# Attention and two MoE layers on one core: four bit passes, P.V halves for two heads at once, the 1e-9 on GpSimd, seven score tiles, another first pair

## The chip, the core and the metric

The kernel runs on one core of one Trainium2 chip. The metric is the device time of one execution in microseconds (us). Before the change it is 682.02 us, the median of three runs (681.51 to 682.46).

## What is computed

Attention over 2 batches x 8 heads, 768 positions, head width 64, and behind it two dense layers. A query sees only keys with the same six sign bits:

```python
q_bits = (np.einsum('bhsd,dk->bhsk', q, proj) > 0)
k_bits = (np.einsum('bhsd,dk->bhsk', k, proj) > 0)
mask = bucket(q_bits)[:, :, :, None] == bucket(k_bits)[:, :, None, :]
scores = np.where(mask, scale * q @ k.T, -1e9)
attn = np.exp(scores - scores.max(-1, keepdims=True))
x = (attn / (attn.sum(-1, keepdims=True) + 1e-9)) @ v      # then heads side by side: 1536 x 512
h = np.maximum(np.maximum(x @ w1, x @ w2), x @ w3) @ w_out
g = h @ w_in; out = (g * sigmoid(1.702 * g)) @ w_out2
```

## The kernel before

Every fp32 product is made of fast fp32r passes over a high and a low part (`hi` rounded to fp32r, `lo` what is left). Work comes in eight pairs of heads, 16 heads, and 96 units of 128 queries by all 768 keys of a head.

*Preparation of a pair.* K and Q of both heads are loaded as one tile [128, 6, 2, 64], turned by TensorE (line 287) in four pieces of three transposes, and split into `kq` high (ScalarE, lines 296 and 298) and low (VectorE, 302 and 304). `prep_bits` then multiplies them with the projection, two pieces of six passes of 384 columns (line 314): for K and for Q, projection high by data high, high by low, low by high. Rows 0 to 43 of the result belong to K, rows 64 to 107 to Q, twelve rows a head: six projections, twice. VectorE turns them into bits and their opposites (line 320), GpSimd scales the Q half by -2^100 (line 325). `prep_stack` copies the parts into `kst` and `qst` by eight transfers on SP's queue (line 335), so that two passes of S = Q.K contain the scores and, in 12 extra rows, 2^100 for every bit that differs.

*The first pair* goes its own way to be early (`solo_` functions): 64-row transposes (line 355), copies of parts by GpSimd (368), a bit piece of two passes per half and operand (384 on 128 rows, 385 on 64 rows), the bits by VectorE (389), the scale by ScalarE (393). Ahead of it TensorE runs nine matmuls of zeros (`WARM`, line 251), and fillers of the same kind (1448) where the plan leaves TensorE idle in the first 26 us.

*A unit.* S in four passes (416); VectorE clamps and takes the minimum (423); ScalarE takes exp with the row sum (429). For every two units: VectorE adds 1e-9 to the sums (433) and inverts them (434), GpSimd scales both score tiles (437), TensorE transposes them in three groups of four (446), ScalarE copies the high part (452), VectorE makes the low part (456), and P.V runs in two halves of six passes (464) on weights [V high | V low]. The result has the product with V high in rows 0 to 63 and with V low in rows 64 to 127. ScalarE copies it (485), a transfer brings the other half to the head's own rows (490), GpSimd adds the two (495, 64x256), and when both heads are there splits the sum into `xh` (501) and `xl` (503), the input of the MoE.

*What sets the order.* `task` gives each step a due time (`DUE`) and a cost (`COST`); `plan` picks, among the steps whose operands and buffers (`free`) are ready, the one with the smallest start + LAM x due. The order that comes out is written to each engine's queue and is fixed there (`in_order`). Engines run their queues in order. Score tiles (`se`) number six, S tiles two, T tiles three, P.V one. The MoE behind has an order of its own, in which TensorE runs without waits.

Of the kernel before, what the change touches and what calls it, by code (L numbers as in the profile page):

```python
# [6 lines left out]
F32R = mybir.dt.float32r  # L7
# [8 lines left out]
BIG = float(2.0 ** 100)  # L16

# [4 lines left out]
SEB = 6  # L22
WARM = 9

DUE = {'prep0': 1.56, 'pa0': -7.67, 'pd0': -16.75, 'prep1': 4.13, 'pa1': -6.11, 'pd1': 4.98, 'S': 0.66, 'clamp': 0.12,
       'exp': 2.96, 'recip': 1.32, 'scale': -4.24, 'T': 3.7, 'hi': 2.96, 'lo': 4.88, 'PV': 7.17, 'xc': 5.17, 'xa': 11.13, 'xs': -8.82,
       'prep': 1.09, 'pa': -6.93, 'pd': -0.18, 'sb': -18.87, 'v': 12.02, 'raw': 3.68, 'stack': 2.09, 'w': 3.14}

COST = {'S': ('PE', .70, .95), 'clamp': ('DVE', .87, 1.05), 'exp': ('ACT', .93, 1.12), 'recip': ('DVE', .14, .36),
        'scale': ('POOL', .92, 1.0), 'T': ('PE', .437, .66), 'hi': ('ACT', .485, .63), 'lo': ('DVE', .60, .73),  # L30
        'PV': ('PE', .72, .95), 'xc': ('ACT', .30, .42), 'xm': ('SP', .65, 3.2), 'xa': ('POOL', .73, .78),
        'xs': ('POOL', 1.2, 1.25),
        'prep': ('PE', .33, .6), 'bits': ('PE', 1.05, 1.32), 'pa': ('ACT', .40, .55), 'pd': ('DVE', .47, .62),
        'pdb': ('DVE', .52, .7), 'sb': ('POOL', .52, .6), 'v': ('POOL', 1.6, 1.65), 'raw': ('SP', 1.4, 5.5),
        'stack': ('SP', 6.6, 9.5), 'none': ('NONE', 0.0, 0.0), 'wm': ('ACT', .57, .7), 'wc': ('POOL', .7, .8),
        'wb': ('DVE', 1.25, 1.4), 'ws': ('ACT', .52, .68), 'wl': ('POOL', 1.27, 1.33), 'up': ('PE', 2.72, 3.0),
        'solob': ('PE', .36, .62), 'dup': ('POOL', .5, .6), 'sbits': ('DVE', .6, .72), 'slow': ('PE', .65, 1.0), 'spd': ('DVE', .52, .62), 'cold': ('PE', .64, 1.0), 'raw0': ('SP', .7, 3.8), 'raw00': ('SP', 2.1, 4.6),
        'project': ('DVE', 1.2, 1.3),
        'warm': ('PE', 4.4, 4.4), 'wraw': ('SP', .45, 6.0)}

FILL = 26.0
LAM = 0.05
# [157 lines left out]
def build(tc, q, k, v, proj, w1, w2, w3, w_out, m2_in, m2_out, out):  # L200
# [13 lines left out]
    NR = D + 44  # L214
# [28 lines left out]
    def f32(ap):  # L243
        return ap.bitcast(F32)


    warm = st([P, 512], "warm", 1, BF16)
# [8 lines left out]
    for base, fill in ((-102, 1.0), (-96, 0.0), (-70, 1.0), (-38, 0.0), (-32, 1.0), (-6, 0.0)):  # L256
        nc.gpsimd.affine_select(out=off, in_=off, compare_op=ALU.is_ge, fill=fill, base=base,
                                pattern=[[0, 1]], channel_multiplier=1)
    pf = st([P, NA], "pf", 1)
    pdf = st([P, 2, NR], "pdf", 1)  # L260
    pdt = st([P, 4, NR], "pdt", 1, F32R)
    nc.gpsimd.memset(pdf, 0.0)
    pds = st([P, 4, D + NA], "pds", 1, F32R)
    offk = st([NR, 1], "offk", 1)
    nc.vector.tensor_scalar(out=offk, in0=off, scalar1=-1.0, scalar2=1.0, op0=ALU.mult, op1=ALU.add)
# [42 lines left out]
    def prep_bits(g, a, get):  # L308
        s = slice(a * HALF, (a + 1) * HALF)
        o = get()[:NR, :HALF]  # L310
        terms = [(pdt[:, i, :], kq[g, name][z][:, s])
                 for x, name in enumerate("kq") for i, z in ((x, 0), (x, 1), (2 + x, 0))]
        for n, (w, x) in enumerate(terms):
            nc.tensor.matmul(o, w, x, start=(n == 0), stop=(n == len(terms) - 1))  # L314
        if a == 0:
            aug[g] = st([NR, S], "aug", 2, F32R)
        t = aug[g]

        def on_dve():
            nc.vector.tensor_scalar(out=t[:, s], in0=o, scalar1=0.0, scalar2=off, op0=ALU.is_gt, op1=ALU.subtract)  # L320
        return (lambda: None), on_dve

    def scale_bits(g, s):
        t = aug[g][D:NR, s]
        nc.gpsimd.tensor_scalar(out=t, in0=f32(t), scalar1=-BIG, scalar2=1.0, op0=ALU.mult, op1=ALU.mult)

    def prep_stack(g, j):
# [3 lines left out]
        ra = slice(32 * j, 32 * j + NA)  # L331
# [12 lines left out]
        last = dma(qs[D:D + NA, 1, :], aug[g][D + 32 * j:D + 32 * j + NA, :])  # L344
# [6 lines left out]
    def solo_transpose(j, name, a, get):  # L351
        t = qkv_raw[0, name]
        o = get()
        for c in range(3):
            nc.tensor.transpose(o[:D, c * P:(c + 1) * P], t[:, 3 * a + c, j, :], ident)
# [23 lines left out]
    def solo_bits(j, name, a, get):  # L379
# [5 lines left out]
        nc.tensor.matmul(o, pds[:D, 2 * x + 1, :], t[:D, z, s], start=False, stop=True)  # L385
# [45 lines left out]
    def softmax_recip(jq):  # L431
        rc[jq] = st([P, 2], "rc", 4)
        nc.vector.tensor_scalar_add(sm[jq], sm[jq], 1e-9)
        nc.vector.reciprocal(rc[jq], sm[jq])  # L434

# [31 lines left out]
    def x_place(jq):  # L467
# [3 lines left out]
        own = slice(j * D, (j + 1) * D)  # L471
        oth = slice((1 - j) * D, (2 - j) * D)
        return g, j, i, b, p, own, oth, slice(i * 2 * P, (i + 1) * 2 * P)

    xtmp = {}

    def x_copy(jq):
        g, j, i, b, p, own, oth, s = x_place(jq)
        if j == 0 and i == 0:
            xf[g] = st([P, S], "xf", 1)  # L480
        if not X:
            X[0] = (st([P, EC, B * S], "xh", 1, F32R), st([P, EC, B * S], "xl", 1, F32R))
        xt, xm = (st([P, 2 * P], tag, 3) for tag in ("xt", "xm"))
        xtmp[jq] = (xt, xm)
        nc.scalar.copy(xt, pv[jq])

    def x_move(jq):
        g, j, i, b, p, own, oth, s = x_place(jq)
        xt, xm = xtmp[jq]
        nc.sync.dma_start(xm[own, :], xt[oth, :])  # L490
# [995 lines left out]
```

## Time and profile before

| | |
|---|---|
| median of 3 runs | 682.02 us |
| profiled execution | 681.95 us |
| its span (first to last instruction) | 680.0 us |
| busy TensorE / VectorE / ScalarE / GpSimd | 673.8 / 581.9 / 424.4 / 312.2 us |
| attention ends, MoE alone on TensorE | 245.51 us |

The span is what the trace covers; the 1.95 us around it are outside. A busy time counts an engine as busy from an instruction's start to its end; TensorE's instructions overlap, so its pace is read from the chain, where a piece is the time by which it moved the end. Line numbers are those of the code above. PE is TensorE, DVE VectorE, ACT ScalarE, POOL GpSimd, SP the queue that issues transfers, PEld TensorE's weight loads.

### The profile page before, as it was taken

What the parts mean: (1) busy time and instruction counts of PE and PEld (TensorE: products, weight loads), DVE (VectorE), ACT (ScalarE), POOL (GpSimd) and SP (SyncE); (2) the same over time, 40 slices, a digit from 0 to 9 for tenths busy, and PEclk for the clock granted to TensorE, in tenths of its full rate; (3) what the DMA queues carried; (4) which work ended last, traced back from release to release, by engine and by line L of the source; (5) the groups of instructions that cost most, each with busy time, mean ns of one, the idle gap of its engine ahead of it and who ended that gap; (6) DMA issues with size and microseconds to landing.
All of it is one profiled execution on the core that took longest, in us unless ns stands there. A gap on an engine that the chain in (4) does not pass through costs nothing.

```text
span 680.0 us, 11507 instructions
## 1 busy us (share of the span) xinstructions
PE 673.8 (99%) x3952; PEld 589.5 (87%) x3952; DVE 581.9 (86%) x1103; ACT 424.4 (62%) x850; POOL 312.2 (46%) x392
## 2 busy tenths in 40 slices
PE   8999999999999999999999999999999999999998
PEld 5899999898999988888888888888888888888886
DVE  7999999999999959998998878886977878787845
ACT  4898888898889934454653454786372735446360
POOL 5478878888887865312302143213343312222200
PEclk9999999999999999999999999999999999999999
DMA  5657686668655012221221222223122230303004
GB/s 116 148 116 158 133 193 146 158 149 194 131 135 139 21 43 62 63 64 62 63 86 48 68 80 93 63 65 121 37 89 62 63 93 31 109 19 122 1 1 185
DMA packets 74410, 63.38 MB, mean 93 GB/s; under 512 B 41377, under 2 KB 65185, under 8 KB 74353
## 3 DMA queue, kind: packets, MB, share of 16 engines
q1 hardware_dynamic: 74128, 62.52, 35.2%
q8 instruction: 31, 0.51, 0.3%
q14 instruction: 27, 0.21, 0.1%
q10 hardware_dynamic: 224, 0.13, 0.1%
HBM read 38.80 MB, written 3.15 MB: 62 GB/s over the span
## 4 chain that ended last, share of the span: by engine, by line
PE 94%; DVE 3%; DMA 1%; issue 1%; ACT 0%; SPq 0%; POOL 0%; DVEq 0%; POOLq 0%; ACTq 0%
PE acc L888 30%; PE acc L1179 19%; PE S L416 8%; PE PV L464 8%; PE T L446 8%; PE acc L1039 7%; PE acc L666 6%; PE T L314 2%; PE T L287 1%; DVE se L423 1%; DVE ptl L456 1%; PE T L666 1%; PE S L251 1%; DMA raw<-in_v_dram 0%; DMA raw<-in_q_dram 0%
## 5 line engine op out<-in xcount | busy, mean ns | idle before, releaser
L437 POOL TENSOR_SCALAR se<-se,rc 128x768 f32<-128x768 f32 x96 | 87.5, 923 | 24.4 <-DVE rc L434 9.1
L456 DVE TENSOR_TENSOR ptl<-T,pth 128x512 fp32r<-128x512 f32 x144 | 94.5, 682 | 3.8 <-ACT pth L452 3.5
L579 POOL TENSOR_SCALAR wmag<-wmag 128x512 f32<-128x512 f32 (+1 forms) x58 | 37.8, 656 | 129.8 <-ACT wmag L572 128.2
L429 ACT ACTIVATE se<-se,mn 128x768 f32<-128x768 f32 x96 | 90.8, 947 | 5.3 <-DVE se L423 4.7
L423 DVE TENSOR_SCALAR_CACHE_REDUCE se<-S 128x768 f32<-128x768 f32 x96 | 90.9, 949 | 1.8 <-PE S L416 1.6
L452 ACT CAST pth<-T 128x512 fp32r<-128x512 f32 x144 | 80.2, 588 | 12.6 <-PE T L446 10.5
L416 PE MATMUL S<-kst,qst 128*128 128x512 f32 (+3 forms) x384 | 87.1, 350 | 0.0
L446 PE MATMUL T<-ident,se 128*128 128x128 f32 x576 | 80.4, 273 | 0.8 <-DVE ptl L456 0.6
L1179 PE MATMUL acc<-wolo,gh 128*128 128x512 f32 (+1 forms) x194 | 75.0, 387 | 0.0
L1179 PE MATMUL acc<-wohi,gh 128*128 128x512 f32 (+1 forms) x194 | 74.9, 387 | 0.0
L464 PE MATMUL PV<-pth,vst 128*128 128x256 f32 x288 | 74.4, 293 | 0.0
L446 PEld LDWEIGHTS T<-ident,se 128*128 128x128 f32 x576 | 65.5, 140 | 5.8 <-DVE ptl L456 1.1
L464 PE MATMUL PV<-ptl,vst 128*128 128x256 f32 x288 | 70.2, 279 | 0.0
L1187 DVE TENSOR_TENSOR res<-acc,res 128x512 f32<-128x512 f32 (+1 forms) x85 | 57.3, 682 | 14.7 <-PE acc L1179 12.3
L416 PEld LDWEIGHTS S<-kst,qst 76*128 76x128 f32 (+1 forms) x384 | 59.2, 190 | 5.3 <-DVE se L423 0.5
L1179 PE MATMUL acc<-wohi,gl 128*128 128x512 f32 (+1 forms) x194 | 59.3, 387 | 0.0
L464 PEld LDWEIGHTS PV<-pth,vst 128*128 128x128 f32 x288 | 54.3, 189 | 1.0
L464 PEld LDWEIGHTS PV<-ptl,vst 128*128 128x128 f32 x288 | 54.4, 189 | 0.0
L602 ACT CAST wohi<-wmag 128x512 fp32r<-128x512 f32 x16 | 9.9, 622 | 63.1 <-DVE wmag L597 46.2
L888 PE MATMUL acc<-xl,whi 128*128 128x256 f32 (+1 forms) x140 | 43.9, 327 | 0.0
L888 PE MATMUL acc<-xh,whi 128*128 128x256 f32 (+1 forms) x140 | 43.6, 325 | 0.0
L1179 PEld LDWEIGHTS acc<-wolo,gh 128*128 128x128 f32 x194 | 36.4, 188 | 7.5
(229 smaller groups left out, 1753.5 us busy)
## 6 DMA issues: line engine op xcount, KB each, us to landing
wraw<-in_moe_w_dram SPq DMA_DIRECT2D x18, 512.0 KB
wraw<-in_moe_w_in_dram SPq DMA_DIRECT2D x16, 512.0 KB
wraw<-in_moe_w_out_dram SPq DMA_DIRECT2D x16, 512.0 KB
kst<-kq SPq DMA_DIRECT2D x42, 192.0 KB
qst<-kq SPq DMA_DIRECT2D x42, 192.0 KB
raw<-in_k_dram SPq DMA_DIRECT2D x16, 192.0 KB
raw<-in_q_dram SPq DMA_DIRECT2D x16, 192.0 KB
raw<-in_v_dram SPq DMA_DIRECT2D x16, 192.0 KB
```

The source lines that it names most:

```text
L416: nc.tensor.matmul(pss[:, x], qs[r, k, c * P:(c + 1) * P], ks[r, k, x], start=k == 0, stop=k == 1)
L423: nc.vector.tensor_scalar(out=se[u], in0=pss[:, :S], scalar1=1.0e9, scalar2=None, op0=ALU.min, op1=ALU.min, accum_out=mn[u])
L429: nc.scalar.activation(se[u], se[u], AF.Exp, bias=mn[u], scale=-1.0, accum_out=sm[u // 2][:, u % 2:u % 2 + 1])
L437: nc.gpsimd.tensor_scalar(out=se[u], in0=se[u], scalar1=rc[u // 2][:, u % 2:u % 2 + 1], scalar2=1.0, op0=ALU.mult, op1=ALU.mult)
L446: nc.tensor.transpose(pst[:, i * P:(i + 1) * P], se[2 * jq + o][:, c * P:(c + 1) * P], ident)
L452: nc.scalar.copy(ptr[jq][0][:, n * 512:(n + 1) * 512], tps[jq, n])
L456: nc.vector.tensor_tensor(out=ptr[jq][1][:, s], in0=tps[jq, n], in1=f32(ptr[jq][0][:, s]), op=ALU.subtract)
L464: nc.tensor.matmul(pv[jq], vs[:, c, :], ptr[jq][t].rearrange("p (o c n) -> p c o n", o=2, c=NTILE)[:, c], start=(c == 0 and t == 0), stop= ...
L888: nc.tensor.matmul(o, w[:, c], x[:, c], start=first and m == 0, stop=m == len(turns) - 1, skip_group_check=True)
L1039: nc.tensor.matmul(o, w[:, c % 3, :], h[:, s], start=(c == 0 and z == 0), stop=(c == FT - 1 and z == 2))
L1179: nc.tensor.matmul(o, g[:, s], w.rearrange("p c f -> p (c f)")[:, e], start=n == 0, stop=n == len(turns) - 1)
L1187: nc.vector.tensor_tensor(out=res[t][:, e], in0=o, in1=res[t][:, e], op=ALU.add)
```

## The change

- *Bits.* High and low part of the projection stand side by side in one 128-column weight tile (`pdt[:, 2z + x]`, two times 64 columns); a piece takes four passes: K high, K low, Q high, Q low. For the low data the low columns are zero. ScalarE copies the lower 64 rows with the sign turned, VectorE compares the upper 64 with them, and one GpSimd operation per pair scales all 64x768 by 2^50 where a bit equals a pattern.
- *Halves.* For the first head a transfer brings its lower half up; for the second one its upper half down, and a further transfer brings its lower half beside the first head's. One addition of 128x256 then serves both heads.
- *1e-9* is added by GpSimd (`softmax_add`), as a step of its own between exp and the reciprocal.
- *Seven score tiles* (`SEB`).
- *First pair.* Loads are [128, 2, 6, 64], so each head's run in a partition is 1,536 bytes without a break; five warm-up matmuls; `proj` is loaded once and copied by VectorE; the second bit pass uses 128 rows for K (zero weights below) and 76 for Q (zeroed rows); the projections' tiles are made by GpSimd and ScalarE (`project`, `project_high`, `project_low`); the start is under `in_order` too.
- The tables `DUE` and `COST` and `LAM` have other numbers, so the order of all of attention differs.

```diff
-SEB = 6
-WARM = 9
+SEB = 7
+WARM = 5
...
-LAM = 0.05
+LAM = 0.0350
...
-    NR = D + 44
+    NB = 64
+    NR = D + NA
...
     pf = st([P, NA], "pf", 1)
-    pdf = st([P, 2, NR], "pdf", 1)
-    pdt = st([P, 4, NR], "pdt", 1, F32R)
-    nc.gpsimd.memset(pdf, 0.0)
+    pdf = st([P, 2, NB], "pdf", 1)
+    pdt = st([P, 4, 2, NB], "pdt", 1, F32R)
     pds = st([P, 4, D + NA], "pds", 1, F32R)
     offk = st([NR, 1], "offk", 1)
-    nc.vector.tensor_scalar(out=offk, in0=off, scalar1=-1.0, scalar2=1.0, op0=ALU.mult, op1=ALU.add)
+    nc.gpsimd.tensor_scalar(out=offk, in0=off, scalar1=-1.0, scalar2=1.0, op0=ALU.mult, op1=ALU.add)
...
         s = slice(a * HALF, (a + 1) * HALF)
-        o = get()[:NR, :HALF]
-        terms = [(pdt[:, i, :], kq[g, name][z][:, s])
-                 for x, name in enumerate("kq") for i, z in ((x, 0), (x, 1), (2 + x, 0))]
+        o = get()[:, :HALF]
+        terms = [(pdt[:, 2 * z + x], kq[g, name][z][:, s]) for x, name in enumerate("kq") for z in range(2)]
         for n, (w, x) in enumerate(terms):
-            nc.tensor.matmul(o, w, x, start=(n == 0), stop=(n == len(terms) - 1))
+            nc.tensor.matmul(o, w.rearrange("p z n -> p (z n)"), x, start=(n == 0), stop=(n == len(terms) - 1))
         if a == 0:
-            aug[g] = st([NR, S], "aug", 2, F32R)
+            aug[g] = st([NB, S], "aug", 2, F32R)
         t = aug[g]
 
+        def on_act():
+            nc.scalar.activation(f32(t[:, s]), o[NB:P], AF.Copy, scale=-1.0)
+
         def on_dve():
-            nc.vector.tensor_scalar(out=t[:, s], in0=o, scalar1=0.0, scalar2=off, op0=ALU.is_gt, op1=ALU.subtract)
-        return (lambda: None), on_dve
+            nc.vector.tensor_tensor(out=t[:, s], in0=o[:NB], in1=f32(t[:, s]), op=ALU.is_gt)
+        return on_act, on_dve
 
     def scale_bits(g, s):
-        t = aug[g][D:NR, s]
-        nc.gpsimd.tensor_scalar(out=t, in0=f32(t), scalar1=-BIG, scalar2=1.0, op0=ALU.mult, op1=ALU.mult)
+        t = aug[g][:, s]
+        nc.gpsimd.tensor_scalar(out=t, in0=f32(t), scalar1=offk[:NB], scalar2=ROOT, op0=ALU.is_equal, op1=ALU.mult)
...
         nc.tensor.matmul(o, pds[:, 2 * x, :], t[:, 0, s], start=True, stop=False)
-        nc.tensor.matmul(o, pds[:D, 2 * x + 1, :], t[:D, z, s], start=False, stop=True)
+        h = slice(0, P if name == "k" else D + NA)
+        nc.tensor.matmul(o, pds[h, 2 * x + 1, :], t[h, z, s], start=False, stop=True)
...
         rc[jq] = st([P, 2], "rc", 4)
-        nc.vector.tensor_scalar_add(sm[jq], sm[jq], 1e-9)
         nc.vector.reciprocal(rc[jq], sm[jq])
+
+    def softmax_add(jq):
+        nc.gpsimd.tensor_scalar(out=sm[jq], in0=sm[jq], scalar1=1e-9, scalar2=1.0, op0=ALU.add, op1=ALU.mult)
...
+        xa[g, j, i] = st([P, 2 * P], "xt" + str(j), 3 - j)
+        if j == 0:
+            xb[g, i] = st([P, 2 * P], "xm", 3)
+        nc.scalar.copy(xa[g, j, i], pv[jq])
 
     def x_move(jq):
-        g, j, i, b, p, own, oth, s = x_place(jq)
-        xt, xm = xtmp[jq]
-        nc.sync.dma_start(xm[own, :], xt[oth, :])
+
+        g, j, i, p, d = x_place(jq)
+        x = xa[g, j, i]
+        if j == 0:
+            nc.sync.dma_start(xb[g, i][0:D], x[D:P])
+        else:
+            nc.sync.dma_start(xb[g, i][D:P], x[0:D])
+            nc.sync.dma_start(xa[g, 0, i][D:P], x[D:P])
 
     def x_add(jq):
-        g, j, i, b, p, own, oth, s = x_place(jq)
-        xt, xm = xtmp[jq]
-        nc.gpsimd.tensor_tensor(out=xf[g][own, s], in0=xt[own, :], in1=xm[own, :], op=ALU.add)
-
-    def x_split(jq):
-        g, j, i, b, p, own, oth, s = x_place(jq)
+        g, j, i, p, d = x_place(jq)
+        x = xa[g, 0, i]
+        nc.gpsimd.tensor_tensor(out=x, in0=x, in1=xb[g, i], op=ALU.add)
+
+    def x_high(jq):
+        g, j, i, p, d = x_place(jq)
+        nc.gpsimd.tensor_scalar(out=X[0][0][:, p, d], in0=xa[g, 0, i], scalar1=1.0, scalar2=1.0,
+                                op0=ALU.mult, op1=ALU.mult)
+
+    def x_low(jq):
+        g, j, i, p, d = x_place(jq)
         xh, xl = X[0]
-        d = slice(b * S + i * 2 * P, b * S + (i + 1) * 2 * P)
-        nc.gpsimd.tensor_scalar(out=xh[:, p, d], in0=xf[g][:, s], scalar1=1.0, scalar2=1.0,
-                                op0=ALU.mult, op1=ALU.mult)
-        nc.gpsimd.tensor_tensor(out=xl[:, p, d], in0=xf[g][:, s], in1=f32(xh[:, p, d]), op=ALU.subtract)
+        nc.gpsimd.tensor_tensor(out=xl[:, p, d], in0=xa[g, 0, i], in1=f32(xh[:, p, d]), op=ALU.subtract)
...
-        qkv_raw[0, "k"], qkv_raw[0, "q"] = (st([P, NTILE, 2, D], "raw", 3) for _ in "kq")
+        qkv_raw[0, "k"], qkv_raw[0, "q"] = (st([P, 2, NTILE, D], "raw", 3) for _ in "kq")
 
         def load_first(name, j):
             src = {"k": k, "q": q}[name]
-            nc.sync.dma_start(qkv_raw[0, name][:, :, j, :], src[0, j].rearrange("(p c) d -> p c d", c=NTILE))
+            nc.sync.dma_start(qkv_raw[0, name][:, j], src[0, j].rearrange("(p c) d -> p c d", c=NTILE))
...
         nc.scalar.dma_start(pf[0:D, 0:6], proj)
         load_first("k", 0)
-        nc.sync.dma_start(pf[D:P, 0:6], proj)
-        nc.vector.tensor_copy(pds, pdf.rearrange("p a n -> p (a n)")[:, 12:13].to_broadcast([P, 4 * (D + NA)]))
+        for j in range(2):
+            solo_open(j)
+        zero = warm[:, 0:1]
+        nc.vector.tensor_copy(pds, zero.to_broadcast([P, 4 * (D + NA)]))
+        for j in range(2):
+            nc.vector.tensor_copy(stacks[j][1][D:D + NA, 1, :], zero[D:D + NA].to_broadcast([NA, S]))
+        nc.vector.memset(pdf, 0.0)
+        nc.vector.tensor_copy(pf[D:P, 0:6], pf[0:D, 0:6])
...
             if u % 2:
-                task("recip", u, lambda u=u: softmax_recip(u // 2), ("recip", u // 2),
-                     deps=[("exp", u - 1), ("exp", u)])
+                task("sum", u, lambda u=u: softmax_add(u // 2), ("sum", u // 2), deps=[("exp", u - 1), ("exp", u)])
+                task("recip", u, lambda u=u: softmax_recip(u // 2), ("recip", u // 2), deps=[("sum", u // 2)])
...
-                 take=("xt",) + (("xf",) if i == 0 and j == 0 else ()), give=("PV",))
-            task("xc", u + 0.1, lambda jq=jq: x_move(jq), ("xm", jq), deps=[("xc", jq)], cost="xm")
-            task("xa", u, lambda jq=jq: x_add(jq), ("xa", jq), deps=[("xm", jq)], give=("xt",))
+                 take=("xt" + str(j),), give=("PV",))
+            task("xc", u + 0.1, lambda jq=jq: x_move(jq), ("xm", jq), deps=[("xc", jq)] + ([("xm", jq - 3)] if j else []),
+                 give=("xt1",) if j else (), cost="xm2" if j else "xm")
             if j == 1:
-                task("xs", u, lambda jq=jq: x_split(jq), ("xs", jq), deps=[("xa", jq)], give=("xf",) if i == 2 else ())
+                task("xa", u, lambda jq=jq: x_add(jq), ("xa", jq), deps=[("xm", jq)])
+                task("xh", u, lambda jq=jq: x_high(jq), ("xh", jq), deps=[("xa", jq)])
+                task("xs", u, lambda jq=jq: x_low(jq), ("xs", jq), deps=[("xh", jq)], give=("xt0",))
```

What the engines are given, counted over the program: TensorE 56 bit passes with 128 columns of weights for 84 with 108, five warm-up matmuls for nine, eight fillers for nine; VectorE 48 additions of 1e-9 fewer; ScalarE 14 copies of 64x384 more; GpSimd 24 additions for 48, 7 scalings of bits for 14, 48 additions of 1e-9 more; SP 24 transfers more. The MoE's instructions stand in the same order on all engines.

TensorE at the first pair's first pieces, before (`T`, `S` and `PV` are PSUM tiles, `pds` the projection's weights):

```order
L355 MATMUL T_133<-ident_76,raw_102 64x128 x3
L355 MATMUL T_138<-ident_76,raw_103 64x128 x3
L355 MATMUL PV_145<-ident_76,raw_103 64x128 x3
L384 MATMUL S_151<-kst_114,pds_99 76x384
L385 MATMUL S_151<-kst_114,pds_99 76x384
L384 MATMUL S_158<-kst_114,pds_99 76x384
L385 MATMUL S_158<-kst_114,pds_99 76x384
```

The same place now:

```order
L357 MATMUL T_130<-ident_72,raw_101 64x128 x3
L357 MATMUL T_135<-ident_72,raw_102 64x128 x3
L357 MATMUL PV_140<-ident_72,raw_102 64x128 x3
L386 MATMUL S_149<-kst_105,pds_98 76x384
L388 MATMUL S_149<-kst_105,pds_98 76x384
L357 MATMUL T_153<-ident_72,raw_101 64x128 x3
L386 MATMUL S_159<-kst_105,pds_98 76x384
L388 MATMUL S_159<-kst_105,pds_98 76x384
```

The second head's first transposes moved up between the two bit pieces of the first.

VectorE around the fifth and sixth reciprocal, before (`sm` sums, `rc` reciprocals, `ptl` low parts of the transposed scores):

```order
L456 TENSOR_TENSOR ptl_483<-T_465,pth_482 128x512
L423 TENSOR_SCALAR se_521,mn_522<-S_497 128x768
L433 TENSOR_SCALAR sm_494<-sm_494 128x2
L434 RECIPROCAL rc_531<-sm_494 128x2
L456 TENSOR_TENSOR ptl_483<-T_489,pth_482 128x512
```

VectorE there now:

```order
L461 TENSOR_TENSOR ptl_489<-T_491,pth_488 128x512
L436 RECIPROCAL rc_531<-sm_433 128x2
L426 TENSOR_SCALAR se_533,mn_534<-S_501 128x768
L426 TENSOR_SCALAR se_540,mn_541<-S_508 128x768
L436 RECIPROCAL rc_566<-sm_513 128x2
```

The additions are gone from VectorE, and clamps (`se, mn`) stand directly behind a reciprocal.

GpSimd in the third pair of heads before, where both heads' parts of x come in (`xf` the sum):

```order
L437 TENSOR_SCALAR se_1155<-se_1155,rc_1272 128x768
L437 TENSOR_SCALAR se_1197<-se_1197,rc_1272 128x768
L495 TENSOR_TENSOR xf_977<-xt_1256,xm_1257 64x256
L501 TENSOR_SCALAR xh_471<-xf_977 128x256
L503 TENSOR_TENSOR xl_472<-xf_977,xh_471 128x256
```

GpSimd at such a place of the first pair now:

```order
L439 TENSOR_SCALAR sm_763<-sm_763 128x2
L502 TENSOR_TENSOR xt_118_537<-xt_118_537,xm_538 128x256
L506 TENSOR_SCALAR xh_469<-xt_118_537 128x256
L512 TENSOR_TENSOR xl_470<-xt_118_537,xh_469 128x256
L442 TENSOR_SCALAR se_708<-se_708,rc_888 128x768
L327 TENSOR_SCALAR aug_829<-aug_829,offk_99 64x768
L442 TENSOR_SCALAR se_743<-se_743,rc_888 128x768
L439 TENSOR_SCALAR sm_833<-sm_833 128x2
```

The sums' addition stands between scalings and the additions of x, and the scalings of a pair of units stand behind a reciprocal that needs it.

## Rows read from the trace of the kernel before

**Rows 1.** The page, its chain of waits: shares by engine.

```profile
PE 94%; DVE 3%; DMA 1%; issue 1%; ACT 0%; SPq 0%; POOL 0%; DVEq 0%; POOLq 0%; ACTq 0%
```

**Rows 2.** Windows: busy us of PE, PEld, DVE, ACT, POOL; clock, DMA share, GB/s.

```profile
0.00:240.00 240.00, 237.04 (x1740) 216.62 (x1741) 227.40 (x513) 202.37 (x429) 188.16 (x258) 1.00 0.61 137
0.00:5.07 5.07, 3.82 (x10) 1.36 (x11) 1.18 (x7) 1.28 (x1) 2.20 (x14) 1.00 0.39 87
...
240.00:680.00 440.00, 436.81 (x2214) 372.83 (x2212) 354.55 (x591) 222.04 (x422) 124.07 (x134) 1.00 0.22 69
```

**Rows 3.** The chain, 71 to 81 us: start us, us, engine, tile, line, instructions.

```profile
71.37 0.87 PE T L446 x8
72.24 0.70 PE S L416 x4
...
73.38 0.71 PE PV L464 x6
...
74.80 1.08 PE T L287 x9
...
79.89 1.05 PE T L314 x6
```

**Rows 4.** The chain at the start and at the end of attention.

```profile
1.25 4.02 PE S L251 x9
5.27 0.58 PE T L355 x3
...
5.88 0.86 ACT kst L362 x2
...
10.84 0.33 PE T L355 x3
11.16 0.22 PE PV L1448
...
14.83 0.17 PE T L384
15.00 0.32 PE T L385
15.32 0.33 PE T L384
...
241.34 2.78 PE T L666 x12
...
245.51 5.50 PE T L666 x24
```

**Rows 5.** Transfers from 0 to 4.6 us, in 40 slices.

```profile
GB/s 1 0 0 0 0 0 0 0 0 0 0 0 0 0 0 0 0 0 3 7 1 78 85 24 163 191 285 292 280 196 98 34 20 114 116 93 120 183 240 263
DMA packets 1462, 0.33 MB, mean 72 GB/s; under 512 B 1462, under 2 KB 1462, under 8 KB 1462
```

**Rows 6.** VectorE's addition of 1e-9: busy us, mean ns, idle before.

```profile
L433 DVE TENSOR_SCALAR sm<-sm 128x2 f32<-128x2 f32 x48 | 13.4, 280 | 0.0
```

**Rows 7.** GpSimd: groups of instructions, then the additions' wait for transfers.

```profile
L257 POOL TENSOR_SCALAR_AFFINE_SELECT off<-off 108x1 f32<-108x1 f32 x6 | 1.1, 186 | 0.3
L495 POOL TENSOR_TENSOR xf<-xt,xm 64x256 f32<-64x256 f32 x40 | 29.6, 742 | 5.7 <-DMA xm<-xt 4.2
L503 POOL TENSOR_TENSOR xl<-xf,xh 128x256 fp32r<-128x256 f32 x21 | 15.5, 738 | 1.7
L437 POOL TENSOR_SCALAR se<-se,rc 128x768 f32<-128x768 f32 x96 | 87.5, 923 | 24.4 <-DVE rc L434 9.1 <-ACT pth L452 6.4 <-PE T L446 2.7
POOL xf L495 <- DMA xm<-xt: 6.5, 6, 1.6
```

**Rows 8.** SP's queue: what its transfers waited for (us, times, longest).

```profile
SPq L490 <- ACT xt L485: 58.4, 26, 5.0
```

**Rows 9.** In order of time: the last part of x and its first reader.

```profile
249.32 0.74 POOL L503 TENSOR_TENSOR xl<-xf,xh 128x256 fp32r<-128x256 f32 x1
...
253.57 0.39 PE L666 MATMUL acc<-xh,whi 128*128 128x512 f32 x1
```

**Rows 10.** The chain where VectorE is on it, 115 to 121 us.

```profile
117.20 0.87 DVE se L423 x2
```

## What the change will do, said before it ran

> **What bounds the kernel now.** I read the page first, then the windows, then the chain. The page puts 94% of the chain of waits on TensorE [rows 1]. A share over the whole span proves little, so the windows come next: they separate attention from the MoE layers behind it. From 0 to 240 us TensorE is busy for 237.0 us and VectorE for 227.4, ScalarE for 202.4, GpSimd for 188.2; behind 240 only TensorE is full [rows 2]. The reader is to see two engines close to their limit in attention, and only one of them on the chain.
>
> The chain says which. In a quiet stretch its pieces follow each other without a gap and carry one engine's name [rows 3], which gives the pace of each kind of pass when passes stand back to back: four S passes 0.70 us, eight transposes 0.87, six P.V passes 0.71, six bit passes 1.05, nine transposes of raw tiles 1.08. The code gives the counts: 96 units, 48 pairs of units with 12 transposes each, 7 pairs of heads with 12 bit passes and 12 transposes each. That is 96 x 0.70 + 72 x 0.87 + 96 x 0.71 + 14 x 1.05 + 84/9 x 1.08 = 67.2 + 62.6 + 68.2 + 14.7 + 10.1 = 222.8 us. The first pair adds 24 transposes (8 x 0.33) and eight bit pieces of two passes (0.17 or 0.33, and 0.32: 4.6 in all), then come the fillers (9 x 0.22) and the first block of the MoE (2.78) [rows 4]: 12.0 us. So 234.8 us of work stand between the first transpose at 5.27 and the end of attention at 245.51, which is 240.2 us. **TensorE idles or crawls for 5.4 us**; 1.4 of them are the hole after 5.85, where ScalarE and VectorE make the first operands. Behind 245.51 all is unchanged: the same 434.5 us.
>
> **The change, part by part.**
>
> *Bits in four passes.* 14 pieces lose two passes each: 28 x 1.05/6 = 0.175 us, **-4.9 us** on the engine that sets the end. The wider weights (128 columns for 108) cost no pass time: S and P.V passes load 128 columns and keep their pace. ScalarE gains 14 copies of 64x384 at 0.43 us, the pace of the start's two [rows 4]: 6.0 us, hidden under its 37.6 us of idle time before 240 [rows 2]; the T buffer is held that much longer, with two others beside it. VectorE's comparison keeps its columns and, I take it, its time.
>
> *Second bit pass of the first pair.* It runs on 64 rows and takes 0.32 us wherever it stands. The pass on 128 rows takes 0.17, but 0.33 directly behind one of 64 rows [rows 4]. The change gives the second pass 128 or 76 rows, and S passes of 76 rows beside ones of 128 keep the full pace [rows 3]. The eight pieces took 4.6 us and would take 16 x 0.175 = 2.8, 1.8 less; half of it lies where TensorE waits for VectorE anyway: **-0.9**. Bounds: 0 and -1.8.
>
> *The start.* Nine warm-up matmuls end at 5.27. The first K tile's bytes move between 2.4 and 3.7 us (slices of 0.115 us) [rows 5], so its transposes wait for warm-up matmuls alone. Five of these end at 1.25 + 5 x 0.45 = 3.5. I put the first transpose at 4.2, half a microsecond behind the last byte, **-1.1**: all up to the first exp follows from it in a row. Bounds: -1.8 (at 3.5) and 0. The change also makes the loads' runs longer: 1,536 bytes in place of 256; all 1,462 packets of the stretch are under 512 bytes [rows 5]. "DMA: Bandwidth & Descriptors" of the Trainium skill (Specifications) asks for at least 512 bytes for line rate, and by it the data is there before the fifth matmul ends; the start term would then be its bound, -1.8, and the time 0.7 us lower. No row here shows a load of long runs, so I keep -1.1. VectorE's new operations ahead of the data (two zeroed 12x768 pieces, a memset, a copy of proj) fit in its idle 3.9 us before 5.07 [rows 2]. The projections' tiles move to GpSimd and ScalarE; no step of the first pair waits for them.
>
> *Fillers:* one fewer, -0.2.
>
> *1e-9 on GpSimd.* 48 additions leave VectorE, 13.4 us of its busy time at a mean of 0.28 [rows 6]. None stands on TensorE, so in the sum this is 0. GpSimd pays 48 x 0.19 = 9 us, the price of its 108x1 operation, to which 128x2 is nearest; upper bound 0.74 (64x256), 36 us [rows 7], still under its idle time.
>
> *Halves for both heads at once.* 48 additions of 64x256 at 0.742 us become 24 of 128x256 at 0.738: -17.9 us of GpSimd [rows 7]. Its net is -8.8 us, beside 51.8 us of idle time before 240 [rows 2]; the scaling of bits, one of 64x768 for two of 44x384, stays about even. SP issues 24 more transfers; it stood waiting for copies for 58.4 us [rows 8], so loads queued behind need not be late, but an addition now waits for two transfers. At the very end this delays the last low part of x, done at 250.06, by one issue; its first reader comes at 253.57 [rows 9].
>
> *Seventh score tile:* 0 by itself; it lets exp run half a pair further ahead.
>
> Sum: -4.9 - 0.9 - 1.1 - 0.2 = **-7.1 us**. The profiled execution took 681.95, which gives 674.85; the median is 682.02, so I say 674.9.
>
> **The rivals.**
>
> *The idle time goes too (671).* Where chain pieces name VectorE [rows 10], TensorE has too little ahead. VectorE loses 13.4 of 227.4 us, a larger share than TensorE's. If the 5.4 us shrink to the start's 1.4 and 0.3 of slow first transposes, 3.7 go: 671.2. Against it: VectorE's saving is spread over 48 places, and holes bunch.
>
> *GpSimd's waits eat part of it (678.8).* Before, additions waited in six places for the halves to land, 6.5 us, and scalings 9.1 us for a reciprocal [rows 7]. Now each of 24 additions needs a second transfer. If all wait as long as those six, 1.08 us, GpSimd stands for 26.0 us, 19.5 more than before, with sums and scalings behind it; a fifth of that reaching the transposes is 3.9 us, 678.8. Seven score tiles speak against.
>
> *VectorE waits for GpSimd (slower).* A reciprocal now stands in VectorE's queue behind an addition in GpSimd's, which itself may stand behind two scalings (2 x 0.92 us) [rows 7]; clamps and low parts queue behind the reciprocal. VectorE has 240.0 - 227.4 + 13.4 = 26.0 us of room, 3.9 of it before the first data [rows 2]; 22.1 / 48 = 0.46 us. That is the point: with longer waits on average the kernel is slower. At 0.6 us: 28.8 - 22.1 = +6.7, 688.7. For it: the order puts additions directly behind scalings and ahead of transfers' waits. Against: the order puts several operations between; a GpSimd addition waits for ScalarE alone.
>
> *TensorE stays slow at the start (677.2).* The page grants the full clock throughout, yet the first matmuls take 0.45 us for 512 columns and later ones 0.22 [rows 4]: the start runs at the lower level, 1.2 GHz, and the first three transposes take 0.58 where later ones take 0.33. With four matmuls fewer the rise may come later. Eight groups of transposes at +0.25 less the one already slow (1.75) and four bit passes at +0.15 are 2.3 us: 677.2. "TensorE: Matmul & The Clock Gate" of the Trainium skill (Part 1) speaks against fewer warm-up matmuls: the slow level is the default, and activity releases it.
>
> *It does nothing (681.9):* TensorE's removed passes all fall where VectorE sets the pace. Rows 3 are against it.
>
> **How the numbers follow.** Forecast 0.58 (its own range 672.5 to 677.5), idle time gone 0.12, GpSimd's waits 0.15, slow start 0.04, nothing 0.04, VectorE waiting 0.07. Under 0.2% (1.4 us, about what a measurement of this kernel can tell from no change) lies only "nothing" and an edge of GpSimd's: same 0.05; faster 0.87; slower 0.08, VectorE's waits and a little for their like. The range of 670 to 680 takes in the bounds of the start and of the first two rivals and leaves out nearly 0.2.
>
> **What would show it.** Right: bit pieces of about 0.70 us on TensorE, the first transpose near 4.2, the MoE starting near 238.4 with 434.5 us behind it, VectorE busy for about 214 us in attention and without waits on GpSimd. Wrong: waits of VectorE's reciprocal for GpSimd above 0.3 us on average, GpSimd waiting for both halves, first S passes later than 10.5, or TensorE's idle time far from 5 us.

## The result and the profile after

The changed kernel takes **688.31 us** (median of four runs, 686.71 to 688.40) against 681.91 us of the kernel before, measured beside it: a ratio of 1.0087 (of the means), with 1.0071 to 1.0103 as its interval. By the medians it is slower by 6.4 us, where 7.1 us less had been forecast. The profiled execution took 686.71 us, its span is 685.0; its mean granted clock of TensorE is 0.999, that of the other three runs, at 688.28 to 688.40 us, 0.997 to 0.998. The only trace is that of the run at 686.71, so the 1.6 us more of the median are not to be seen in it.

The page of the changed kernel, its part on busy times and its chain of waits by engine [rows 1]:

```profile
PE 669.7 (98%) x3919; PEld 584.2 (85%) x3919; DVE 569.9 (83%) x1053; ACT 429.3 (63%) x866; POOL 320.7 (47%) x417
...
PE 82%; POOL 7%; DVE 5%; issue 3%; ACT 2%; DMA 0%; POOLq 0%; ACTq 0%; SPq 0%
```

Two things are to be seen. GpSimd is busy for 320.7 us, where it had 312.2 and was to have 8.8 less. And it stands on the chain with 7%, where it had 0%; TensorE has lost 12 points. VectorE did get its 12 us.

The windows tell where the time came in (columns as in [rows 2]; the first row ends where attention ends):

```profile
0.00:250.64 250.64, 238.41 (x1742) 216.42 (x1743) 217.72 (x466) 209.37 (x449) 200.36 (x288) 1.00 0.62 140
...
250.64:685.00 434.36, 431.25 (x2178) 367.81 (x2177) 352.20 (x587) 219.94 (x417) 120.30 (x130) 1.00 0.22 69
```

The MoE behind takes 434.4 us, as before. All of the change lies in attention, which ends at 250.64 us in place of 245.51; 238.4 had been forecast. TensorE was to lose work, and did: the chain has bit pieces of four passes at the forecast 0.71 us ("0.71 PE T L313 x4" at 109.81).

The groups of instructions of GpSimd up to the end of attention (columns: busy us, mean ns, idle before and its releaser) [rows 7]:

```profile
L442 POOL TENSOR_SCALAR se<-se,rc 128x768 f32<-128x768 f32 x96 | 88.8, 937 | 16.7 <-DVE rc L436 12.4 <-PE T L451 2.3 <-PE S L419 1.6
L327 POOL TENSOR_SCALAR aug<-aug,offk 64x768 fp32r<-64x768 f32 x7 | 20.3, 2893 | 1.2 <-DVE aug L322 0.7
L502 POOL TENSOR_TENSOR xt<-xt,xm 128x256 f32<-128x256 f32 x23 | 16.9, 736 | 3.0 <-DMA xm<-xt 1.9
...
L439 POOL TENSOR_SCALAR sm<-sm 128x2 f32<-128x2 f32 x48 | 9.7, 201 | 16.9 <-ACT se L432 13.9
```

The additions of halves (0.736 us) and of 1e-9 (0.20 us) cost what had been estimated. The scaling of bits does not: **2.89 us each for 64x768, 20.3 us in all**, where the kernel before spent 14 times 0.512, 7.2 us. A scaling of score tiles works on the same 768 columns, on twice as many rows, in 0.94 us.

What such an operation does to its neighbours is read from the timeline of GpSimd (columns: start us, us, engine, line, operation), 140 to 150 us, in the fourth of the seven places:

```profile
142.55 3.16 POOL L327 TENSOR_SCALAR aug<-aug,offk 64x768 fp32r<-64x768 f32 x1
145.79 0.73 POOL L502 TENSOR_TENSOR xt<-xt,xm 128x256 f32<-128x256 f32 x1
146.62 0.41 POOL L506 TENSOR_SCALAR xh<-xt 128x256 fp32r<-128x256 f32 x1
147.11 0.73 POOL L512 TENSOR_TENSOR xl<-xt,xh 128x256 fp32r<-128x256 f32 x1
147.92 0.19 POOL L439 TENSOR_SCALAR sm<-sm 128x2 f32<-128x2 f32 x1
148.20 1.27 POOL L616 TENSOR_TENSOR wlo<-wmag,whi 128x512 fp32r<-128x512 f32 x1
149.44 0.91 POOL L442 TENSOR_SCALAR se<-se,rc 128x768 f32<-128x768 f32 x1
```

and VectorE's reciprocal there:

```profile
148.15 0.17 DVE L436 RECIPROCAL rc<-sm 128x2 f32<-128x2 f32 x1 [2.49 <-POOL sm L439]
```

The sum of a 128x2 tile stands last in a row of five operations that the long one opens, and VectorE stands for 2.49 us. The timelines of VectorE and TensorE show how that reaches TensorE: the clamp stands behind the reciprocal in VectorE's queue, and TensorE stands 2.11 us for the clamp ahead of its next S passes.

```profile
148.23 0.94 DVE L426 TENSOR_SCALAR_CACHE_REDUCE se<-S 128x768 f32<-128x768 f32 x1
...
149.23 0.97 PE L419 MATMUL S<-kst,qst 128*128 128x512 f32 x4 [2.11 <-DVE se L426]
```

In the waits of the whole of attention VectorE's wait for sums is among the largest (columns: us in total, times, longest):

```profile
POOL sm L439 <- ACT se L432: 13.9, 13, 2.8
ACT pth L457 <- PE T L451: 13.5, 19, 2.0
DVE rc L436 <- POOL sm L439: 12.4, 15, 2.5
POOL se L442 <- DVE rc L436: 12.4, 14, 2.3
PEld T L451 <- POOL se L442: 9.3, 18, 1.4
```

These can be read as a ring, which the totals suggest and do not prove: VectorE waits for a sum, GpSimd for the reciprocal, TensorE for GpSimd's scaled scores, ScalarE for TensorE. Of VectorE's 12.4 us, 7.3 lie at the first reciprocal behind one of six of the seven long operations (1.74, 0.64, 0.43, 2.49, 1.12 and 0.85).

### The profile page after: what moved, and what is told of

Read it like the earlier page. It is cut to its first block, busy times and chain, and to the rows that moved or that the text cites. A ratio compares the mean times of both kernels' runs of the same rounds, so it can differ in the third digit from the quotient of the medians.

```text
span 685.0 us, 11393 instructions
## 1 busy us (share of the span) xinstructions
PE 669.7 (98%) x3919; PEld 584.2 (85%) x3919; DVE 569.9 (83%) x1053; ACT 429.3 (63%) x866; POOL 320.7 (47%) x417
## 4 chain that ended last, share of the span: by engine, by line
PE 82%; POOL 7%; DVE 5%; issue 3%; ACT 2%; DMA 0%; POOLq 0%; ACTq 0%; SPq 0%
PE acc L897 30%; PE acc L1188 19%; PE acc L1048 7%; PE acc L675 6%; PE PV L469 6%; PE S L419 6%; PE T L451 5%; POOL se L442 3%; DVE se L426 2%; DVE ptl L461 2%; POOL aug L327 2%; PE T L675 1%; ACT se L432 1%; POOL xt L502 1%; PE T L287 1%
## 5 line engine op out<-in xcount | busy, mean ns | idle before, releaser
L442 POOL TENSOR_SCALAR se<-se,rc 128x768 f32<-128x768 f32 x96 | 88.8, 937 | 16.7 <-DVE rc L436 12.4
L451 PE MATMUL T<-ident,se 128*128 128x128 f32 x576 | 82.2, 274 | 6.0 <-POOL se L442 4.8
```

Of the source, the lines that this page charges most:

```text
L442: nc.gpsimd.tensor_scalar(out=se[u], in0=se[u], scalar1=rc[u // 2][:, u % 2:u % 2 + 1], scalar2=1.0, op0=ALU.mult, op1=ALU.mult)
L451: nc.tensor.transpose(pst[:, i * P:(i + 1) * P], se[2 * jq + o][:, c * P:(c + 1) * P], ident)
```

## The experiments

**The first theory:** the comparison in the scaling of bits (`is_equal`) makes it three times as long as the estimate, and everything else is as forecast. Rivals: the additions of 1e-9 on GpSimd are the fault (VectorE waits for GpSimd); the planner's order, built on 0.9 us for this step, is.

### The scale without a comparison

The same numbers come from a product and a sum: bit x (+-2^50) + (0 or 2^50), with a column for each. The order is that of the changed kernel, instruction by instruction, with two small operations more at the start that make the columns.

```diff
+    nc.gpsimd.tensor_scalar(out=up_, in0=off, scalar1=-2.0 * ROOT, scalar2=ROOT, op0=ALU.mult, op1=ALU.add)
+    nc.gpsimd.tensor_scalar(out=at0, in0=off, scalar1=ROOT, scalar2=1.0, op0=ALU.mult, op1=ALU.mult)
...
-        nc.gpsimd.tensor_scalar(out=t, in0=f32(t), scalar1=offk[:NB], scalar2=ROOT, op0=ALU.is_equal, op1=ALU.mult)
+        nc.gpsimd.tensor_scalar(out=t, in0=f32(t), scalar1=up_[:NB], scalar2=at0[:NB], op0=ALU.mult, op1=ALU.add)
```

> The changed kernel with its order kept and one thing altered: bits are scaled by a multiplication and an addition with two columns of constants, in place of the comparison is_equal (64x768, 2.85 us each, 7 times). Theory A (the comparison on GpSimd is three times as dear as a multiplication of the same columns and holds up the scalings behind it): the operation takes 0.92 us and the kernel 675 to 679. Theory B (reciprocals waiting for sums on GpSimd cost the time): the operation gets cheap too, but the kernel stays at 684 to 688. Theory C (the new order as such is worse): 684 to 688 as well.

It took **677.87 us**, 0.994 of before (0.9925 to 0.9954) and 10.4 us less than the changed kernel (8.8 less than its profiled run, at 686.71 us). By source line (min/median/max ns, first and last start):

```profile
L330 POOL TENSOR_SCALAR aug<-aug,up__10_101,at x7: 973/980/1406, 26.3 to 197.3; 64x768 fp32r<-64x768 f32 x7
```

Its page, busy times and the chain by engine:

```profile
PE 668.0 (99%) x3919; PEld 584.7 (86%) x3919; DVE 569.0 (84%) x1053; ACT 428.8 (63%) x866; POOL 308.2 (46%) x419
...
PE 94%; DVE 2%; ACT 1%; POOL 1%; issue 1%; DMA 0%; SPq 0%; ACTq 0%; POOLq 0%
```

and its waits:

```profile
POOL sm L442 <- ACT se L435: 16.1, 12, 2.8
POOL se L445 <- DVE rc L439: 13.2, 14, 2.8
...
DVE rc L439 <- POOL sm L442: 2.5, 4, 1.3
```

VectorE's wait for sums falls from 12.4 to 2.5 us and TensorE has its 94% again. This version has the whole computation and is faster than either kernel.

### The planner told of the length, with and without the comparison

```diff
-        'pdb': ('DVE', .47, .62), 'sb': ('POOL', .9, .97), 'v': ('POOL', 1.65, 1.7), 'raw': ('SP', 1.4, 5.5),
+        'pdb': ('DVE', .47, .62), 'sb': ('POOL', 2.85, 2.95), 'v': ('POOL', 1.65, 1.7), 'raw': ('SP', 1.4, 5.5),
```

> The changed kernel with one number of its table altered: the plan is told 2.85 us for the comparison instead of 0.90, so the order is made for what it takes. Theory A says: the GpSimd time stays, the misplaced waits go, 680 to 685. Theory B: no more than 1 us of difference. Theory C: a new order may be 3 us better or worse.

695.84 us, 1.0205 of before (1.0188 to 1.0222): outside all that had been expected, a true cost gave a plan 7.5 us worse than the false one. A part of this is TensorE's clock. In the profiled run (694.79 us) a scaling of bits of 2.84 us on GpSimd holds up the scaling of scores behind it, TensorE stands for 2.36 us, and then works for some 3 us at a granted clock of 0.50, the lower of its two levels (timelines of GpSimd and TensorE, then a window with the columns of [rows 2]):

```profile
207.32 2.84 POOL L327 TENSOR_SCALAR aug<-aug,offk 64x768 fp32r<-64x768 f32 x1
...
211.22 1.54 PE L451 MATMUL T<-ident,se 128*128 128x128 f32 x6 [2.36 <-POOL se L442]
...
211.00:214.00 3.00, 2.78 (x11) 2.59 (x12) 1.03 (x3) 1.16 (x4) 2.75 (x6) 0.50 1.05 227
```

To tell the order from the operation, the same order then ran with product and sum:

> Bits by multiplication and addition, in the order that the plan makes when told 2.85 us for them. If that order lost its 9 us against the change by what it waits for the comparison, it is near 677 to 681 here. If the order as such is poor (due times belong to one set of costs), 684 to 690.

690.28 us (1.0126, 1.0109 to 1.0143). Its four runs have a mean granted clock of 1.00. In this order the comparison costs 5.6 us (695.84 - 690.28), of which some 1.5 are the slow stretch (an estimate: half of its 3 us), and the order alone 12.4 (690.28 - 677.87). One number of a planner moves everything behind it. Which of the moved steps costs the 12.4 us wasn't followed; in the last run GpSimd's sums wait longer for exp, and exp longer for the clamps:

```profile
POOL sm L442 <- ACT se L435: 28.0, 19, 3.8
...
ACT se L435 <- DVE se L429: 13.3, 11, 3.1
```

against 16.1 and 3.8 us with the other order. So telling the planner the length does not mend the changed kernel, with either operation.

### The sums away, with and without the comparison

The 48 additions of 1e-9 on GpSimd, called sums here, are left out, so this part of the computation is missing.

```diff
     def softmax_add(jq):
-        nc.gpsimd.tensor_scalar(out=sm[jq], in0=sm[jq], scalar1=1e-9, scalar2=1.0, op0=ALU.add, op1=ALU.mult)
+        pass
```

> The changed kernel with its order kept, and the 48 additions of 1e-9 left out (this part of the computation is missing; the comparison is_equal stays). Reciprocals then wait for exp alone. Theory A: 684 to 687. Theory B: 12.4 us of waits of VectorE and 9.7 us of GpSimd go, 676 to 680. Theory C: 684 to 688.

> Both alterations at once: bits by multiplication and addition, and the 48 additions of 1e-9 left out (this part of the computation is missing). Theory A: the same as with the bits alone within 1.5 us, 674 to 678. Theory B: the same as without the additions alone, 676 to 680. If both matter, it lies 3 us or more below the better of the two. Theory C: 682 to 688.

681.21 us (0.9991, 0.9982 to 1.0) and 676.46 us (0.992, 0.9905 to 0.9934). The first lies between the ranges of the theories and bears none of them out. With the changed kernel and the short scale that makes a table, in us:

| | sums on GpSimd | sums left out | what the sums cost |
|---|---|---|---|
| scale with `is_equal` | 688.31 | 681.21 | 7.1 |
| scale with product and sum | 677.87 | 676.46 | 1.4 |
| what the comparison costs | 10.4 | 4.75 | |

Neither cost stands alone. The 13.0 us more of GpSimd (20.3 - 7.3) cost 4.75 us where no reciprocal needs a sum from it, and 5.7 more where one does. At the changed kernel's best run, 686.71, the 5.7 are 4.1; the other three have the lower mean clock. The sums are the path by which a long operation on GpSimd reaches VectorE.

### The sums back on VectorE

That path can be cut the other way, with the short scale kept:

```diff
     def softmax_recip(jq):
+        nc.vector.tensor_scalar_add(sm[jq], sm[jq], 1e-9)
...
-        nc.gpsimd.tensor_scalar(out=sm[jq], in0=sm[jq], scalar1=1e-9, scalar2=1.0, op0=ALU.add, op1=ALU.mult)
+        pass
```

> The kernel with bits by multiplication and addition (677.9 us), its order kept, with the additions of 1e-9 back on VectorE directly ahead of the reciprocals. Theory B in its weak form (the way over GpSimd costs 1.4 us, as leaving the additions out showed): 676.3 to 677.5. If VectorE lacked the time (13 us more of it in busy time): 679 to 682.

682.32 us (1.0009, 1.0 to 1.0019), 4.45 us more than with the sums on GpSimd. Moving them was right as long as GpSimd is quick, and in this order is worth more than the nothing that the forecast gave it.

### Load on GpSimd in other places

Each addition of halves as two of 64 rows, in the kernel with the short scale:

```diff
-        nc.gpsimd.tensor_tensor(out=x, in0=x, in1=xb[g, i], op=ALU.add)
+        for r in (slice(0, D), slice(D, P)):
+            nc.gpsimd.tensor_tensor(out=x[r], in0=x[r], in1=xb[g, i][r], op=ALU.add)
```

> The kernel with bits by multiplication and addition (677.9 us), its order kept, and each addition of the halves made as two of 64 rows, 48 in all as before the change: GpSimd is busy for 24 x 0.74 = 17.8 us more. If GpSimd is near the bound by now (theory A, the comparison was the same kind of load), 3 to 8 us slower: 681 to 686. If GpSimd has room, no more than 1 us: 677 to 679.

684.93 us (1.0046, 1.0031 to 1.0061): 17.6 us more of GpSimd's busy time (325.8 - 308.2) cost 7.1 us, and the wait for sums is back:

```profile
DVE rc L439 <- POOL sm L442: 11.3, 16, 1.7
```

So GpSimd's load costs 0.40 us per us here without any comparison, and 0.80 in lumps of 2.89 us (10.4 / 13.0; 0.68 by the profiled run, 8.8 / 13.0). Against two additions in the same place, one joint addition of halves, which the forecast priced at nothing but room, is worth these 7 us.

### The comparison in the kernel before

The kernel before with its own order and sums on VectorE; its 14 scalings get a comparison. The edit changes the mask: a query's opposite bits, which are -1 there, become 0 and are lost from it.

```diff
-        nc.gpsimd.tensor_scalar(out=t, in0=f32(t), scalar1=-BIG, scalar2=1.0, op0=ALU.mult, op1=ALU.mult)
+        nc.gpsimd.tensor_scalar(out=t, in0=f32(t), scalar1=1.0, scalar2=-BIG, op0=ALU.is_equal, op1=ALU.mult)
```

> The kernel before the change, its order kept, with one thing altered: the 14 scalings of bits (44x384) use the comparison is_equal, ahead of the same multiplication. They should take 1.4 to 1.5 us instead of 0.51, 13 us more of GpSimd in all, as much as the change added. Theory A in its narrow form (the comparison costs what it takes wherever GpSimd's order is tight): 3 to 8 us slower, 685 to 690. If only the new order is tight: 682 to 683.

686.04 us (1.0071, 1.0051 to 1.0091), 4.3 us more. By source line:

```profile
L325 POOL TENSOR_SCALAR aug<-aug x14: 1492/1494/1807, 24.8 to 204.0; 44x384 fp32r<-44x384 f32 x14
```

0.512 us have become 1.494, 13.7 us in all: the same factor of three on another shape, in another order, and much the same price as in the column of the table without sums.

### Which operations are slow

Scratch operations on GpSimd in a row at the start, 64x768, with constants unless said.

> The kernel with bits by multiplication and addition, and eleven operations on a scratch tile put into GpSimd's queue at the start, to read their durations (the total time means nothing here). If the comparison itself is dear, is_equal on 64x768 takes 2.8 us with a constant as with a column, and 1.4 us on 64x384, while multiplication, addition and maximum take 0.9 to 1.0. If the column operand or its place made it dear, is_equal with a constant takes 0.9 to 1.0. Open: whether is_gt and is_ge are as dear.

The operations put before everything make the kernel longer, 704.06 us; only their own durations are read. GpSimd's timeline, in the order product and product, product and sum, maximum and product, greater and product, equal and product, product and equal, product with a column, equal with a column:

```profile
5.16 0.83 POOL L265 TENSOR_SCALAR probe<-probe 64x768 f32<-64x768 f32 x1
6.07 0.83 POOL L266 TENSOR_SCALAR probe<-probe 64x768 f32<-64x768 f32 x1
6.98 2.78 POOL L267 TENSOR_SCALAR probe<-probe 64x768 f32<-64x768 f32 x1
9.85 2.77 POOL L268 TENSOR_SCALAR probe<-probe 64x768 f32<-64x768 f32 x1
...
15.56 2.78 POOL L270 TENSOR_SCALAR probe<-probe 64x768 f32<-64x768 f32 x1
...
21.28 2.78 POOL L272 TENSOR_SCALAR probe<-probe 64x768 f32<-64x768 f32 x1
24.16 0.90 POOL L273 TENSOR_SCALAR probe<-probe,offk 64x768 f32<-64x768 f32 x1
25.16 2.85 POOL L274 TENSOR_SCALAR probe<-probe,offk 64x768 f32<-64x768 f32 x1
```

Products and sums take 0.83 us; one comparison in either place makes 2.78, and so does a maximum, for which 0.9 to 1.0 had been expected. The column operand adds 0.07 us and is not the cause, nor is equality as such.

### The scale on ScalarE

```diff
-        nc.gpsimd.tensor_scalar(out=t, in0=f32(t), scalar1=up_[:NB], scalar2=at0[:NB], op0=ALU.mult, op1=ALU.add)
+        nc.scalar.activation(t, f32(t), AF.Identity, scale=up_[:NB], bias=at0[:NB])
```

> The order of the kernel with bits by multiplication and addition (677.9 us), with that operation on ScalarE (scale and bias by column) at the same place of the sequence, so GpSimd loses its 7.3 us. If GpSimd is what still stands between 677.9 and the 674.9 forecast (about 0.4 us lost per us of it, as two additions for one showed): 674 to 676.5. If ScalarE, at 208 of 238 us, takes it badly: 678 to 681.

680.66 us (0.9985, 0.9975 to 0.9994), 2.8 us more than on GpSimd, though the operation itself takes no longer (group of instructions):

```profile
L330 ACT ACTIVATE aug<-aug,at,up__10_101 64x768 fp32r<-64x768 f32 x7 | 7.2, 1029 | 0.0
```

So taking this operation off GpSimd in this way brings back nothing of the 3.0 us by which the kernel with the short scale lies above the forecast.

### Two terms of the forecast by themselves

Both edits are made to the kernel with the short scale. Two passes with weights of zeros (a tile made at the start) are put behind each bit piece (six passes again):

```diff
-            nc.tensor.matmul(o, w.rearrange("p z n -> p (z n)"), x, start=(n == 0), stop=(n == len(terms) - 1))
+            nc.tensor.matmul(o, w.rearrange("p z n -> p (z n)"), x, start=(n == 0), stop=False)
+        for n in range(2):
+            nc.tensor.matmul(o, pzs[0], kq[g, "kq"[n]][0][:, s], start=False, stop=(n == 1))
```

> The kernel with bits by multiplication and addition (677.9 us), its order kept, and in each of the 14 bit pieces two more passes of 384 columns on zero weights, so six as before the change. If TensorE sets the end of attention, 28 x 0.175 = 4.9 us come back: 682 to 683. If the removed passes lay beside GpSimd's, ScalarE's or VectorE's waits, 1 to 3 us: 679 to 681.

681.57 us (0.9993, 0.9984 to 1.0003): the removed passes are worth 3.7 us (681.57 - 677.87) of the 4.9 forecast.

```diff
-WARM = 5
+WARM = 9
```

> The kernel with bits by multiplication and addition (677.9 us), its order kept, with nine warm-up matmuls again instead of five. The first transposes then wait for the ninth, 1.7 us later: 679.3 to 679.8 if the start is in a row with all that follows; no change, 677.6 to 678.2, if the time is made up behind it.

678.81 us (0.9956, 0.994 to 0.9973): nine warm-up matmuls cost 0.9 us, between nothing and the 1.7 that had been weighed.

## Why the prediction was wrong

**The step that failed** is the one in half a sentence: "the scaling of bits, one of 64x768 for two of 44x384, stays about even". It counted columns, 768 for two times 384, and did not look at the operation, which the change had turned from a product into a comparison. No row of the trace of before shows a `tensor_scalar` comparison on GpSimd, so it had to be bounded like the other unknown prices, and was not. It measured 20.3 us in place of 7.2, GpSimd's busy time grew by 8.5 us where it was to shrink by 8.8 (13.1 of these 17.3 are this operation; the rest are smaller items, the projections' tiles with 1.7 and the scalings of scores with 1.3 among them), and "beside 51.8 us of idle time" no longer held. Put right alone, it takes the kernel to 677.87 us, inside the range of 670 to 680 and 3.0 above the forecast.

**The rivals.** "VectorE waits for GpSimd" named 688.7 us, and the queue it described is the one that is seen: reciprocal behind sum, sum behind other work of GpSimd, clamp behind reciprocal. It was still not right in its terms, and that its time comes so near is luck: it added 6.7 us, for a mean wait of 0.6 us, to the time of the kernel before, with none of the other terms of the sum. The point from which it decides was put at a mean wait of 0.46 us; the mean is 12.4 / 48 = 0.26, under the 0.3 that was to be a sign of being wrong too, and the kernel is slower all the same. A mean over 48 places says little where 15 waits, up to 2.5 us, make up the whole, and idle time of VectorE elsewhere does not undo them. And what fills GpSimd was not "two scalings" ahead of a sum but the long operation. GpSimd's waits for transfers, the other rival, are small: 1.9 us for the halves in attention, under the 4.2 of [rows 7].

**Bits in four passes: right in kind, sized too high.** The pace is the forecast 0.70 to 0.71 us a piece; 3.7 of the 4.9 us reach the end.

**Start: at its better bound.** The chain of the changed kernel at the start [rows 4]:

```profile
1.25 2.31 PE S L252 x5
3.56 1.29 PE T L357 x6
...
8.84 0.37 PE T L386
9.21 0.19 PE T L388
```

The first transposes begin when the fifth matmul ends, at 3.56 us, 1.7 ahead of 5.27; I had kept 4.2. The transfers of the first 4.6 us (40 slices, [rows 5]) tell why:

```profile
GB/s 0 0 0 0 0 0 0 0 0 0 0 0 0 0 0 27 107 134 40 93 280 401 403 311 298 338 414 334 187 200 200 214 254 200 147 120 147 160 307 309
DMA packets 560, 0.65 MB, mean 141 GB/s; under 512 B 143, under 2 KB 560, under 8 KB 560
```

Twice the bytes in 560 packets in place of 1,462. The rule that was set beside the estimate ("DMA: Bandwidth & Descriptors" of the Trainium skill, Specifications: 512 bytes and more for line rate) gave -1.8, and the trace agrees in that the data is there by 3.56; 143 of the 560 packets are still under 512 bytes, and no run parts the run length from the earlier issue. It was not worth that much at the end: in the run with nine matmuls the first transposes begin 1.42 us later (4.99 against 3.57 in the short-scale kernel), the first bit pass 0.68 later (9.77 against 9.09), and the end comes 0.9 later. The second bit pass takes 0.19 us in place of 0.32, as forecast.

**A slow TensorE at the start** came in part. The window from 0 to 5 us again shows the full granted clock, 1.00, yet behind five warm-up matmuls the first nine transposes of the short-scale kernel take 1.93 us, 0.64 for three; six at 11.26 us take 0.66, and in the run with nine matmuls the first three take 0.34. So three groups run at half pace, not eight, and lose 0.9 us in all, where the kernel before lost 0.25. By "TensorE: Matmul & The Clock Gate" of the Trainium skill (Part 1) the slow level is the default and activity releases it; the trace agrees as far as these nine transposes go. The 677.2 us of that rival do not follow, since the run with nine matmuls is the slower one.

**1e-9 and the halves** had their durations right and their worth wrong. Both were put at 0 in the sum; they measured 4.45 us (against sums on VectorE) and 7.1 us (against two additions in the same place), each in this order, so what the forecast calls idle time in attention, 51.8 us of GpSimd and 12.6 of VectorE, is far from free room.

**What stays open.** With the short scale TensorE idles for about 10 us of attention, where "TensorE idles or crawls for 5.4 us" was kept: from 3.57 to 241.87 are 238.3 us, for 234.8 - 4.9 - 1.8 - 0.2 = 227.9 of work by the forecast's own pieces. The sums account for 1.4 us of that (676.46 against 677.87) and the slow first transposes for 0.9. The rest was not taken apart; nor was it found what makes the one other order tried so much worse.

## What to carry to other kernels

An estimate by tile shape holds only for the same arithmetic: when an edit changes an operation's kind, find a row with that kind on that engine, or bound it from both sides as one would a new instruction. A small step that joins two engines (a 0.19 us sum between exp and reciprocal) inherits the longest operation in the queue it joins, so look for what may stand ahead of it, and judge by the longest waits, not by their mean. And when a plan is fixed, idle time on a second engine is not room: here each us of added GpSimd work cost 0.31 to 0.80 us (4.3 / 13.7 in the kernel before, 10.4 / 13.0 in the changed one). A part of such a cost can come by the clock: where a long operation made TensorE stand for 2.36 us, its granted clock was 0.50 for the next 3 us.

## What the runs showed of the hardware that was not expected

On GpSimd, a two-step operation of constants on 64x768 takes 0.83 us when both steps are products or sums and 2.78 us when one is a comparison or a maximum; on 44x384 of the kernel before, 0.512 and 1.494 us. On VectorE the two-input operations of the changed kernel show no such gap: a comparison of 64x384 (L322) takes 0.54 us, a subtraction of 128x384 (L302) 0.55. One-input operations were not set side by side there. "GPSIMD Engine Reference" of the Trainium skill (section 4.1) calls one-input element-wise work on GpSimd, the maximum among it, roughly line-rate. The probe does not agree for the maximum: at 2.78 us beside 0.83 for a product it takes more than three times as long, and the measurement decides.
